# Starting one weight fewer before the wide products, and catching up inside them

## Chip, cores and metric

The kernel runs on one core of one Trainium2 chip. The metric is the device time of one execution in microseconds (us). Before the change it is 538.14 us, the median of three runs (537.76 to 539.08).

## What is computed

The reference is an attention with a decaying state, followed by two feed-forward layers on the 1536 tokens that it gives (B = 2, 768 positions, 8 heads of 64, so 512 features):

```python
for b in range(nb):                                  # blocks of 64 positions
    intra = einsum(einsum(qb, kb) * Dmask, vb)
    inter = einsum(qb * lam_pow, kv_state)
    out[:, :, sl] = intra + inter
    kv_state = lam_block * kv_state + einsum(kb_dec, vb)

rms = sqrt(mean(x * x) + 1e-06); xn = x / rms * rms_g     # layer 1: w_gate, w_val 512x1536, w_out 1536x512
x = (silu(xn @ w_gate) * (xn @ w_val)) @ w_out
h = maximum(maximum(x @ w1, x @ w2), x @ w3)              # layer 2: 512x768 each, w_out 768x512
return h @ w_out
```

## The kernel before

**Split weights.** Every large matrix product is made of three: an operand is cut into a high part (`wh`, `xh`) and what is left (`wl`, `xl`), and a product is high by high, high by low and low by high, each a TensorE (PE) matmul of 128x128 by 128x512. A weight is handled in pieces of 128 by 512, called units: `("g", f)` of w_gate, `("v", f)` of w_val, `("o", f)` of w_out; g0 below stands for `("g", 0)`. A unit comes as raw 32-bit words by DMA (`load_to`, L164 to L172: three DMAs for g and v, one for o) and is then made by four engines in turn:

- `begin_unit` (L231): two ScalarE (ACT) operations, `W<-wraw` (L252) and `wraw<-wraw` (L253);
- `words_of_unit` (L204), in three steps: three VectorE (DVE) operations `mid<-W` (L209), `mid<-mid` (L212), `W<-wraw,mid` (L216), and after the third an addition on GpSimd (POOL), `W<-W,wraw` (L219);
- `finish_unit` (L174): the cast `wh<-W` on ACT (L180) and the difference `wl<-W,wh` on POOL (L183). Only now can PE use the unit.

`third_of_unit` (L258) does this as a conveyor: one call in three begins a unit and does the first step of the one before it, the next finishes the one before that and does the second step, the third does the third step.

**Attention first, then mixed with the wide products.** Tokens come in 12 chunks of 128. The manual schedule at the end (L992 to L1018) runs seven turns, `s_` 0 to 6, of attention alone. In a turn the chunk `s_` is transposed (T: `pk`, `pq` on PE, then `kT`, `qT` on ACT), chunk `s_ - 1` gets its scores (C: `sc`, then `A` and the state `S` on DVE), chunk `s_ - 2` its output (M: `px` on PE, `sq` and `x` on ACT; U: `pm`) and chunk `s_ - 3` its scaling (N: `pb` on PE, `x` on DVE, `xh` on ACT; R: `xl` on POOL). The next chunk's `k`, `q`, `v` are loaded at T (`loads_at`, L104), and ahead of them the next unit's raw words (L995, L996). Units are begun at N of the late turns (L998 to L1000), and their steps are put behind b, U and V of the same turn.

After that `first_stage` (L656) begins the wide products of layer 1, for three blocks of 512 tokens: `hidden1` (L621) makes `pg` and `pv` of one f by `proj` (L492, 12 matmuls each), and after two f's `out_two` (L638) makes the four `acc`. The units are wanted in this order: g0, v0, g1, v1, g2, o0, o1, v2, g3, v3, o2, o3. What is left of the attention is spread between these matmuls: every third matmul calls `spread` (L467), directly or by `gap`. `spread` counts its calls in `pos["half"]`; it may call `third_of_unit` once, and then takes the next pieces of attention off their queue. Its first call also finishes the oldest unit and adds the last step of the one after it (L482 to L484). One `proj` has four such places, so g0 has places 1 to 4, v0 5 to 8, and o0 and o1 begin at place 21.

**Later stages.** When the attention is done (`lates`), `gap` (L453) runs the conveyor, and in `second_stage` (L895) products of sums of units (`Tg`, `Tv` and others) run in an order written out by hand.

**Order of waiting.** Each engine carries out its own instructions in the order in which the program emits them, so one that waits holds those behind it. PSUM tiles rotate through eight banks. SyncE (SP) issues all the DMAs of weights and chunks.

The lines touched are L469 in `spread`, and L995 and L998 in the schedule. The line that decides how often the conveyor moves during the first stage is

```python
if not lates and (pos["half"] - 1) % 5 % 3:
    third_of_unit()
```

which calls it at three places of five (the second, third and fifth).

Of the kernel before, what the change touches and what calls it, by code (L numbers as in the profile page):

```python
# [26 lines left out]
def tile_decay_attention_swiglu_maxout(  # L27
# [41 lines left out]
    lates = []  # L69
# [34 lines left out]
    def loads_at(c):  # L104
        if c <= CPNB:
            loads_to(c + 2)
        elif c == CPNB + 1:
            load(c + 1, 2)
        elif c + 1 < NCH:
            for n in range(3):  # L110
                load(c + 1, n)
# [50 lines left out]
    pos = {"load": 0, "made": 0, "raw": 0, "step": 0, "gap": 0, "half": 0, "quiet": False, "lag": 3, "narrow": True, "seam": False}  # L162
# [11 lines left out]
    def finish_unit(key, W, at):  # L174
        if key:
            if second_sum(key):
                W = sums_in.pop((key[0][1], key[1]))
            wh = wpools[at].tile([P, 512], F32R, tag="wh", name="wh")
            wl = wpools[at].tile([P, 512], F32R, tag="wl", name="wl")
            nc.scalar.copy(out=wh, in_=W.bitcast(F32))  # L180
            if second_sum(key):
                return lambda: lower_of_sum(key, W, wh, wl)
            nc.gpsimd.tensor_tensor(out=wl, in0=W.bitcast(F32), in1=wh.bitcast(F32), op=ALU.subtract)  # L183
            units[key] = (wh, wl)
# [73 lines left out]
    def third_of_unit():  # L258

        if not thirds:  # L260
            if pos["seam"] and stage1 and first_sum(stage1[0][0]):
                return
            done = stage2.pop(0) if stage2 else (None,) * 3
            unit = stage1.pop(0) if stage1 else (None,) * 5
            later = []
            thirds.extend([lambda: (begin_unit(), words_of_unit(0, *unit)),
                           lambda: (later.append(finish_unit(*done)), words_of_unit(1, *unit)),
                           lambda: (later[0] and later[0](), words_of_unit(2, *unit), stage2.append(unit[:3]))])
        thirds.pop(0)()
# [20 lines left out]
    def turn(c, scaled=True):  # L290
        kn, qn, vn = qkv[c][0], qkv[c][1], qkv[c][2]
        pk = bank("pk")
        pq = bank("pq")
        pkv = pk.rearrange("p (a t) -> p a t", t=P)
        pqv = pq.rearrange("p (a t) -> p a t", t=P)
        for a in range(NP):
            nc.tensor.transpose(pkv[:, a, :], kn[:, 2 * a:2 * a + 2, :].rearrange("p h d -> p (h d)"), ident)
        for a in range(NP):
            nc.tensor.transpose(pqv[:, a, :], qn[:, 2 * a:2 * a + 2, :].rearrange("p h d -> p (h d)"), ident)
        kT = att.tile([P, NP, P], F32, tag="kT", name="kT", bufs=1)  # L300
        nc.scalar.copy(out=kT, in_=pkv)
        qT = att.tile([P, NP, P], F32, tag="qT", name="qT", bufs=1)
        nc.scalar.copy(out=qT, in_=pqv)
        st[c] = dict(kT=kT, qT=qT, pq=pqv, vn=vn)
        if scaled:
            scaled_queries(c)
        if c == 0:
            decayed_keys(0)
# [26 lines left out]
    def masked(hf):  # L335
        def piece(c):
            d = st[c]
            if hf == 0:
                d["A"] = att.tile([P, H, C], F32, tag="A", name="A", bufs=1)
            nc.vector.tensor_tensor(  # L340
                out=d["A"].rearrange("p (a t) i -> p t a i", t=2)[:, hf],
                in0=d["sc"][hf][:, :HF].rearrange("p (a i) -> p a i", i=C),
                in1=Tm.rearrange("p (a t) i -> p t a i", t=2)[:, hf], op=ALU.mult)
            if hf == 0:
                d["S0"] = last_state[0]
                d["S1"] = next_state(c, 0, d["S0"])
        return piece
# [82 lines left out]
    def rest(c):  # L430
# [6 lines left out]
    named = dict(M=(2, mixed), N=(3, normed), C=(1, scores), a=(1, masked(0)), R=(3, rest),  # L437
                 b=(1, masked(1)), U=(2, summed), V=(1, advance), T=(0, lambda c: (loads_at(c), turn(c))),
                 t=(0, lambda c: (loads_at(c), turn(c, False))), Q=(1, scaled_queries),
                 K=(-1, decayed_keys), k=(0, decayed_keys),  # L440
                 w=(3, lambda c: None))
# [5 lines left out]
    def attn_step():  # L447
        _, fn, c = attn_q.pop(0)
        fn(c)
# [16 lines left out]

    def spread():  # L467
        pos["half"] += 1
        if not lates and (pos["half"] - 1) % 5 % 3:  # L469
            third_of_unit()  # L470
        if gaps[0]:
            left = sum(1 for p in attn_q if p[0] <= gaps[1])
            for _ in range(-(-left // gaps[0])):
                attn_step()
            gaps[0] -= 1
            if not attn_q and not lates:
                att_ctx.close()
                wpools.append(ctx.enter_context(tc.tile_pool(name="wp2", bufs=8)))
                lates.append(ctx.enter_context(tc.tile_pool(name="late", bufs=1)))
                pos["narrow"] = False  # L480
                x_sums()
        if pos["half"] == 1:  # L482
            finish_unit(*stage2.pop(0))
            words_of_unit(3, *split_unit[0])  # L484
# [479 lines left out]
    with tc.manual_schedule():  # L964
        nc.scalar.dma_start(out=lam8, in_=lam.rearrange("(o h) -> o h", o=1).to_broadcast([P, H]))
        loads_to(0)
        for to, src in crosswise(g_sb, rms_g.rearrange("(a p) -> p a", p=P)):
            nc.scalar.dma_start(out=to, in_=src)
        make_identity(nc, ident)
        nc.vector.memset(ones, 1.0)  # L970
        nc.vector.memset(zeros, 0.0)
        nc.scalar.activation(out=mhalf, in_=zeros[:, 0:1], func=AF.Silu)
        nc.vector.memset(mhalf, -0.5)
        warm = bank("warm")
        for i in range(9):
            nc.tensor.matmul(out=warm[:, 0:P], lhsT=zeros, rhs=zeros, start=True, stop=True)
        nc.vector.tensor_tensor(out=diag, in0=ident[:, :C], in1=ident[:, C:], op=ALU.add)
        for hf in range(2):
            nc.vector.tensor_copy(out=lamh[64 * hf:64 * hf + 64, :],
                                  in_=lam8.rearrange("p (a t) -> p t a", t=2)[64 * hf:64 * hf + 64, hf, :])  # L980
        for a in range(NP):
            nc.vector.tensor_tensor_scan(
                out=lami[:, a, :], data0=lamh[:, a:a + 1].to_broadcast([P, C]), data1=zeros[:, :C],
                initial=1.0, op0=ALU.mult, op1=ALU.add)
        for h in range(H):
            nc.vector.tensor_tensor_scan(
                out=Tm[:, h, :], data0=lam8[:, h:h + 1].to_broadcast([P, C]), data1=diag,
                initial=0.0, op0=ALU.mult, op1=ALU.add)
        loads_to(1)
        pos["narrow"] = False  # L990
        unit_ = None
        for s_ in range(CPNB + 3):  # L992
            while attn_q[0][0] == s_:
                fn = attn_q[0][1]
                if s_ and fn in (named["t"][1], named["T"][1]):  # L995
                    load_to(pos["load"] + 1)  # L996
                attn_step()
                if s_ > 2 and fn is named["N"][1]:  # L998
                    begin_unit()
                    unit_ = stage1.pop(0)  # L1000
                if unit_ and s_ == CPNB + 2:
                    if fn is named["U"][1]:
                        words_of_unit(3, *added_later)
                    elif fn is named["V"][1]:
                        for n in range(3):
                            words_of_unit(n, *unit_, split_add=True)
                        split_unit.append(unit_)
                        stage2.append(unit_[:3])
                elif unit_ and fn is named["b"][1]:
                    words_of_unit(0, *unit_)  # L1010
                elif unit_ and fn is named["U"][1]:
                    words_of_unit(1, *unit_)
                    if stage2:
                        finish_unit(*stage2.pop(0))
                elif unit_ and fn is named["V"][1]:
                    words_of_unit(2, *unit_, split_add=s_ == CPNB + 1)
                    added_later = unit_
                    stage2.append(unit_[:3])  # L1018
        begin_unit()
        finish = first_stage()  # L1020
        pos["step"] = len(steps)
        second_stage(finish)
# [31 lines left out]
```

## Time and profile before

| What | Value |
|---|---|
| median of 3 runs | 538.14 us (537.76 to 539.08) |
| profiled execution, its own time | 540.95 us |
| its span, first to last instruction | 539.2 us |
| mean granted TensorE clock | 0.994 of full |
| first wide matmul (`pg`) starts | 38.84 us |
| chain that ended last, share of PE | 84% |

The span is what the trace covers; the time of the same execution is 1.75 us longer. The views used below are the page's top, a table of stretches (busy time of each engine, granted clock as a share of full, DMA), the list of waits, and the instructions of one engine in order of time.

### The profile page before, as it was taken

To read this page: it belongs to the slowest core of one execution; us is meant where nothing else is said; L and a number is where in the kernel's file an instruction comes from. 1 tells how busy PE (TensorE), PEld (TensorE's weight loads), DVE (VectorE), ACT (ScalarE), POOL (GpSimd) and SP (SyncE) were. 2 spreads that over 40 slices of the span, in tenths; PEclk is the share of its full clock that TensorE was granted. 3 is DMA by queue.
4 is the path that set the end of the run, shared out by engine and by line. 5 is a ranking of instruction groups with operands and counts; after the bars stand their busy time and mean duration, and the time that the engine had idled before them with its cause. 6 is when DMAs were issued, how large, how long until landed. Compare 5 with 4: busy or idle time off the path is not lost.

```text
span 539.2 us, 9762 instructions
## 1 busy us (share of the span) xinstructions
PE 528.1 (98%) x3728; PEld 436.1 (81%) x3728; DVE 369.9 (69%) x680; ACT 278.2 (52%) x541; POOL 301.3 (56%) x247
## 2 busy tenths in 40 slices
PE   7989999999999999999999999999999999999997
PEld 6777777788888888888888888888888888888886
DVE  4795786538866677858667676878775587684354
ACT  3776684354463674364455446555466744641120
POOL 2485888334345667457365557985387543951060
PEclk9899999999999999999999999999999999999999
DMA  8989662001112213212131221211024321300014
GB/s 197 233 191 263 182 158 80 2 1 39 40 40 79 78 41 117 74 43 84 57 97 39 78 80 40 80 39 57 32 70 120 114 72 48 103 15 0 1 50 185
DMA packets 65598, 44.67 MB, mean 83 GB/s; under 512 B 40080, under 2 KB 61840, under 8 KB 65552
## 3 DMA queue, kind: packets, MB, share of 16 engines
q1 hardware_dynamic: 64848, 44.05, 28.4%
q8 instruction: 29, 0.48, 0.4%
q14 instruction: 17, 0.14, 0.1%
q10 hardware_dynamic: 704, 0.01, 0.1%
HBM read 40.90 MB, written 3.15 MB: 82 GB/s over the span
## 4 chain that ended last, share of the span: by engine, by line
PE 84%; DVE 1%; POOL 0%; issue 0%; ACT 0%; DVEq 0%
PE p L691 34%; PE acc L882 9%; PE r L691 9%; PE acc L488 6%; PE acc L490 6%; PE acc L489 6%; PE pv L498 5%; PE q L691 4%; PE pg L498 4%; PE px L384 1%; POOL wl L183 0%; PE sc L326 0%; PE sc L331 0%; PE pb L423 0%; DVE S L358 0%
## 5 line engine op out<-in xcount | busy, mean ns | idle before, releaser
L183 POOL TENSOR_TENSOR wl<-W,wh 128x512 fp32r<-128x512 f32 x77 | 102.1, 1326 | 53.1 <-ACT wh L180 53.0
L219 POOL TENSOR_TENSOR W<-W,wraw 128x512 int32<-128x512 int32 x60 | 79.1, 1318 | 75.9 <-DVE W L216 75.6
L180 ACT CAST wh<-W 128x512 fp32r<-128x512 f32 x77 | 47.9, 622 | 75.0 <-POOL W L219 73.7
L509 POOL TENSOR_TENSOR hl<-sg,hh 128x512 fp32r<-128x512 f32 x36 | 47.6, 1322 | 35.9 <-ACT hh L508 35.7
L691 PE MATMUL p<-xh,wh 128*128 128x512 f32 x148 | 57.6, 389 | 0.0
L691 PE MATMUL p<-xl,wh 128*128 128x512 f32 x148 | 57.6, 389 | 0.0
L691 PE MATMUL p<-xh,wl 128*128 128x512 f32 x148 | 57.6, 389 | 0.0
L490 PE MATMUL acc<-hh,wl 128*128 128x512 f32 x144 | 56.3, 391 | 0.5 <-POOL wl L183 0.5
L488 PE MATMUL acc<-hh,wh 128*128 128x512 f32 x144 | 56.7, 394 | 0.0
L489 PE MATMUL acc<-hl,wh 128*128 128x512 f32 x144 | 56.1, 389 | 0.0
L846 DVE TENSOR_TENSOR acc_sb<-acc,acc_sb 128x512 f32<-128x512 f32 x46 | 31.8, 690 | 17.4 <-PE acc L490 16.1
L252 ACT ACTIVATE W<-wraw 128x512 f32<-128x512 f32 x60 | 40.4, 673 | 3.9 <-DMA wraw<-in_moe_w_dram 3.9
L209 DVE TENSOR_SCALAR mid<-W 128x512 f32<-128x512 f32 x58 | 39.7, 684 | 3.3 <-ACT W L252 3.3
L212 DVE TENSOR_SCALAR mid<-mid 128x512 int32<-128x512 int32 x58 | 40.2, 693 | 0.8
L253 ACT ACTIVATE wraw<-wraw 128x512 int32<-128x512 uint32 x60 | 40.1, 669 | 0.0
L216 DVE SCALAR_TENSOR_TENSOR W<-wraw,mid 128x512 int32<-128x512 int32 x58 | 39.4, 679 | 0.9
L746 ACT COPY c<-p 128x512 f32<-128x512 f32 x34 | 19.9, 586 | 38.0 <-PE p L691 37.7
L509 POOL TENSOR_TENSOR hl<-m,hh 128x512 fp32r<-128x512 f32 x18 | 24.1, 1349 | 23.0 <-ACT hh L508 22.9
L691 PE MATMUL p<-yh,wh 128*128 128x512 f32 x90 | 35.0, 389 | 0.0
L691 PE MATMUL p<-yl,wh 128*128 128x512 f32 x90 | 35.0, 389 | 0.0
L691 PE MATMUL p<-yh,wl 128*128 128x512 f32 x90 | 35.0, 389 | 0.0
L508 ACT CAST hh<-sg 128x512 fp32r<-128x512 f32 x36 | 22.3, 620 | 24.0 <-DVE sg L632 16.4
(176 smaller groups left out, 1316.1 us busy)
## 6 DMA issues: line engine op xcount, KB each, us to landing
wraw<-in_moe_w_out_dram SPq DMA_DIRECT2D x18, 512.0 KB, 3.4
wraw<-in_moe_w_dram SPq DMA_DIRECT2D x18, 512.0 KB, 3.6
kn<-in_k_dram SPq DMA_DIRECT2D x12, 256.0 KB, 4.5
qn<-in_q_dram SPq DMA_DIRECT2D x12, 256.0 KB, 5.2
vn<-in_v_dram SPq DMA_DIRECT2D x12, 256.0 KB, 4.9
wraw<-in_moe_w_gate_dram SPq DMA_DIRECT2D x12, 256.0 KB, 3.4
wraw<-in_moe_w_gate_dram SPq DMA_DIRECT2D x24, 128.0 KB, 3.4
wraw<-in_moe_w_val_dram SPq DMA_DIRECT2D x12, 256.0 KB, 3.0
```

The source lines that it names most:

```text
L180: nc.scalar.copy(out=wh, in_=W.bitcast(F32))
L183: nc.gpsimd.tensor_tensor(out=wl, in0=W.bitcast(F32), in1=wh.bitcast(F32), op=ALU.subtract)
L212: nc.vector.tensor_scalar(out=mid[key], in0=mid[key], scalar1=0x07FFFFFF, scalar2=3, op0=ALU.bitwise_and, op1=ALU.logical_shift_left)
L219: nc.gpsimd.tensor_tensor(out=W, in0=W, in1=lo, op=ALU.add)
L252: nc.scalar.activation(out=W.bitcast(F32), in_=hi.bitcast(F32), func=AF.Abs)
L488: nc.tensor.matmul(out=out, lhsT=wh, rhs=xh_, start=first, stop=False)
L489: nc.tensor.matmul(out=out, lhsT=wh, rhs=xl_, start=False, stop=False)
L490: nc.tensor.matmul(out=out, lhsT=wl, rhs=xh_, start=False, stop=last)
L498: nc.tensor.matmul(out=ps, lhsT=w[:, kk * P:(kk + 1) * P], rhs=x[:, kk, :], start=n == 0, stop=n == len(todo) - 1)
L509: nc.gpsimd.tensor_tensor(out=dst_l, in0=src, in1=dst_h.bitcast(F32), op=ALU.subtract)
L691: nc.tensor.matmul(out=ps, lhsT=w[:, ks], rhs=r[:, o + k, :], start=first and k == 0 and n == 0, stop=k == 1 and n == 2, skip_group_check= ...
L882: nc.tensor.matmul(out=acc[:, cs], lhsT=x[:, ts], rhs=w[:, cs], start=n == 0, stop=n == len(todo) - 1)
```

## The change

Two places. In the attention turns the first raw unit is loaded from turn 2 on and not from turn 1 (L995), and units are begun at N of turns 4, 5, 6 and not of 3, 4, 5, 6 (L998); with the one begun behind the turns (L1019), four units are under way when the wide products begin, where there were five. In `spread`, up to the 24th place three of four places call the conveyor (the second, third and fourth); from the 25th on, three of five as before. Of the first 24 places that is 18 calls, where there were 14.

```diff
@@ spread
         pos["half"] += 1
-        if not lates and (pos["half"] - 1) % 5 % 3:
+        if not lates and ((pos["half"] - 1) % 4 if pos["half"] < 25 else (pos["half"] - 1) % 5 % 3):
             third_of_unit()
@@ the schedule
                 fn = attn_q[0][1]
-                if s_ and fn in (named["t"][1], named["T"][1]):
+                if s_ > 1 and fn in (named["t"][1], named["T"][1]):
                     load_to(pos["load"] + 1)
                 attn_step()
-                if s_ > 2 and fn is named["N"][1]:
+                if s_ > 3 and fn is named["N"][1]:
                     begin_unit()
                     unit_ = stage1.pop(0)
```

On PE no instruction moves. On the other engines the order changes from turn 1 on. First place: ACT behind the first two `proj`, before, from the cast of v1 on (`wh_1004<-W_809` is v1, `W_1065` is o1):

```order
L180 CAST wh_1004<-W_809 128x512
L629 ACTIVATE sg_1020<-pg_890 128x512
L301 COPY kT_1052<-pk_1042 128x512
L303 COPY qT_1054<-pq_1043 128x512
L252 ACTIVATE W_1065<-wraw_952 128x512
L253 ACTIVATE wraw_952<-wraw_952 128x512
L395 ACTIVATE sq_1097<-px0_1070 128x256
```

and now, from the cast of g1 on (`W_793` is g1, `W_873` is v1, `W_1024` is o0):

```order
L180 CAST wh_988<-W_793 128x512
L629 ACTIVATE sg_1006<-pg_876 128x512
L252 ACTIVATE W_1024<-wraw_938 128x512
L253 ACTIVATE wraw_938<-wraw_938 128x512
L301 COPY kT_1045<-pk_1035 128x512
L303 COPY qT_1047<-pq_1036 128x512
L180 CAST wh_1054<-W_873 128x512
L395 ACTIVATE sq_1086<-px0_1059 128x256
```

Each unit's cast stands one unit behind, and the cast of v1 now stands ahead of `sq`.

Second place: ACT one chunk later, before (`W_958` is o0) and now (`W_1199` is v2, `W_1024` is o0):

```order
L180 CAST wh_1199<-W_958 128x512
L629 ACTIVATE sg_1194<-pg_1123 128x512
L301 COPY kT_1239<-pk_1229 128x512
L303 COPY qT_1241<-pq_1230 128x512
L508 CAST hh_1246<-sg_1194 128x512
```

```order
L629 ACTIVATE sg_1185<-pg_1109 128x512
L252 ACTIVATE W_1199<-wraw_1020 128x512
L253 ACTIVATE wraw_1020<-wraw_1020 128x512
L180 CAST wh_1208<-W_1024 128x512
L301 COPY kT_1239<-pk_1229 128x512
L303 COPY qT_1241<-pq_1230 128x512
L508 CAST hh_1246<-sg_1185 128x512
```

The cast of o0 stood ahead of `kT` before too; now there is one more unit's begin in front of it.

Third place: POOL over the same chunk, before (`W_887` is g2, `W_958` o0, `W_1065` o1) and now (`W_873` is v1, `W_942` g2, `W_1024` o0, `W_1154` o1):

```order
L435 TENSOR_TENSOR xl_939<-x_798,xh_938 128x4x128
L219 TENSOR_TENSOR W_887<-W_887,wraw_741 128x512
L183 TENSOR_TENSOR wl_1110<-W_887,wh_1109 128x512
L509 TENSOR_TENSOR hl_1120<-sg_1020,hh_1119 128x512
L219 TENSOR_TENSOR W_958<-W_958,wraw_863 128x512
L414 TENSOR_TENSOR diag_82<-diag_82,mhalf_79 128x1
L287 TENSOR_TENSOR kd_1192<-kn_1036,Tm_80 128x512
L183 TENSOR_TENSOR wl_1200<-W_958,wh_1199 128x512
L435 TENSOR_TENSOR xl_939<-x_930,xh_938 128x4x128
L219 TENSOR_TENSOR W_1065<-W_1065,wraw_952 128x512
L509 TENSOR_TENSOR hl_1247<-sg_1194,hh_1246 128x512
L183 TENSOR_TENSOR wl_1309<-W_1065,wh_1308 128x512
```

```order
L219 TENSOR_TENSOR W_873<-W_873,wraw_725 128x512
L435 TENSOR_TENSOR xl_925<-x_782,xh_924 128x4x128
L183 TENSOR_TENSOR wl_1055<-W_873,wh_1054 128x512
L219 TENSOR_TENSOR W_942<-W_942,wraw_847 128x512
L509 TENSOR_TENSOR hl_1106<-sg_1006,hh_1105 128x512
L183 TENSOR_TENSOR wl_1170<-W_942,wh_1169 128x512
L414 TENSOR_TENSOR diag_82<-diag_82,mhalf_79 128x1
L219 TENSOR_TENSOR W_1024<-W_1024,wraw_938 128x512
L287 TENSOR_TENSOR kd_1183<-kn_1029,Tm_80 128x512
L435 TENSOR_TENSOR xl_925<-x_916,xh_924 128x4x128
L183 TENSOR_TENSOR wl_1209<-W_1024,wh_1208 128x512
L219 TENSOR_TENSOR W_1154<-W_1154,wraw_940 128x512
```

From the first `wl` of the wide stretch to that of o1 POOL has 17 operations before and 19 now: one addition and one difference more.

## Rows read from the trace of the kernel before

**Rows 1.** Top of the page: busy us of each engine, share, instructions.

```profile
PE 528.1 (98%) x3728; PEld 436.1 (81%) x3728; DVE 369.9 (69%) x680; ACT 278.2 (52%) x541; POOL 301.3 (56%) x247
```

**Rows 2.** Table of stretches: A:B us; busy (count) by engine; PEclk; DMA; GB/s.

```profile
17.40:18.50 1.10, 0.12 (x11) 0.04 (x4) 0.44 (x1) 1.10 (x4) 0.34 (x1) 1.00 0.80 239
21.00:24.50 3.50, 3.41 (x102) 2.89 (x95) 3.02 (x9) 2.08 (x8) 1.86 (x3) 0.51 0.81 212
24.50:33.00 8.50, 8.28 (x255) 7.36 (x248) 8.23 (x26) 7.70 (x19) 7.65 (x8) 1.00 0.79 185
34.00:38.10 4.10, 3.50 (x69) 2.90 (x69) 3.70 (x12) 3.61 (x10) 3.33 (x4) 1.00 0.75 182
38.10:41.60 3.50, 3.42 (x39) 2.49 (x39) 2.15 (x4) 2.09 (x4) 2.69 (x3) 0.51 0.97 251
46.10:68.00 21.90, 20.82 (x320) 16.30 (x318) 16.06 (x37) 15.19 (x35) 19.52 (x17) 1.00 0.81 223
92.00:539.00 447.00, 443.83 (x2130) 367.03 (x2128) 302.74 (x497) 217.09 (x401) 240.19 (x186) 1.00 0.19 61
```

**Rows 3.** List of PE's waits over the span: us in total, times, longest.

```profile
PE sc L331 <- issue: 1.0, 1, 1.0
PE px L384 <- issue: 0.8, 1, 0.8
PE pq L299 <- DMA qn<-in_q_dram: 0.6, 2, 0.4
PE acc L490 <- POOL wl L183: 0.5, 1, 0.5
PE px L384 <- ACT sg L629: 0.3, 1, 0.3
PE sc L331 <- DMA vn<-in_v_dram: 0.2, 1, 0.2
```

**Rows 4.** PE in order of time: start us, us, instruction, [idle before <- releaser].

```profile
46.65 0.39 PE L498 MATMUL pv<-xh,wl 128*128 128x512 f32 x1
...
49.89 0.28 PE L384 MATMUL px<-qs,S 64*64 64x64 f32 x3 [0.34 <-ACT sg L629]
...
67.99 0.50 PE L490 MATMUL acc<-hh,wl 128*128 128x512 f32 x1 [0.53 <-POOL wl L183]
...
199.00 0.39 PE L691 MATMUL r<-ah,wl 128*128 128x512 f32 x1
```

**Rows 5.** POOL in order of time: two of the differences wl, at 46 and 66 us.

```profile
46.13 1.30 POOL L183 TENSOR_TENSOR wl<-W,wh 128x512 fp32r<-128x512 f32 x1 [5.34 <-ACT wh L180]
...
66.65 1.29 POOL L183 TENSOR_TENSOR wl<-W,wh 128x512 fp32r<-128x512 f32 x1 [0.82 <-ACT wh L180]
```

**Rows 6.** POOL's groups, 46.1 to 67.97 us: count; busy us, mean ns; idle before.

```profile
L183 POOL TENSOR_TENSOR wl<-W,wh 128x512 fp32r<-128x512 f32 x5 | 6.4, 1289 | 7.6 <-ACT wh L180 7.6
L219 POOL TENSOR_TENSOR W<-W,wraw 128x512 int32<-128x512 int32 x4 | 5.2, 1309 | 0.0
L509 POOL TENSOR_TENSOR hl<-sg,hh 128x512 fp32r<-128x512 f32 x2 | 2.6, 1301 | 0.0
L435 POOL TENSOR_TENSOR xl<-x,xh 128x512 fp32r<-128x512 f32 x2 | 2.6, 1290 | 0.0
L287 POOL TENSOR_TENSOR kd<-kn,Tm 128x512 f32<-128x512 f32 x2 | 2.1, 1065 | 0.0
L414 POOL TENSOR_TENSOR diag<-diag,mhalf 128x1 f32<-128x1 f32 x2 | 1.1, 551 | 0.0
```

**Rows 7.** ACT and DVE in order of time, at sq, kT and the reduction.

```profile
51.81 0.68 ACT L395 ACTIVATE sq<-px 128x256 f32<-128x256 f32 x2
...
60.33 0.58 ACT L301 COPY kT<-pk 128x512 f32<-128x512 f32 x1
...
52.51 1.08 DVE L401 TENSOR_REDUCE zeros<-sq 128x128 f32<-128x512 f32 x1 [0.39 <-ACT sq L395]
```

**Rows 8.** POOL in order of time: the difference of unit Tg6, in the second stage.

```profile
193.61 1.30 POOL L183 TENSOR_TENSOR wl<-W,wh 128x512 fp32r<-128x512 f32 x1 [1.49 <-ACT wh L180]
```

## Prediction

> **What bounds the kernel now.** The top of the page comes first: PE is busy 528.1 us of 539.2 [rows 1]. So time can go only where PE stands still or where its clock is low, and the table of stretches says where. From 92 us to the end PE is busy 443.83 of 447.00 us at clock 1.00 [rows 2], with no wait long enough for the list. What can be won or lost lies in the first 92 us, where the change is. There the list of waits [rows 3] holds, beside those of the first 9 us, three kinds. Two stops are put down to "issue", 1.0 and 0.8 us: the engine waits for nothing that the profile shows. Two are for chunks that DMA brings late, 0.4 us for `qn` (the longer of its two) and 0.2 us for `vn`, both shortly ahead of 38.1 us. Two lie among the wide products: 0.34 us at 49.89 for the bank that the silu frees, and 0.53 us at 67.99, when the third matmul with o1 waits for its `wl` [rows 4]. PE is never held by the making of a weight before 38 us. Twice the granted clock is at half, the lower of its two levels (1.2 of 2.4 GHz): 3.5 us from 21.0 and 3.5 us from 38.1, each at 0.51, which costs 0.49 x 3.5 = 1.7 us of PE's work each time. The first follows a stretch with a stop (PE busy 0.12 of 1.10 us from 17.4). The second follows one with several (3.50 of 4.10 us from 34.0). No drop follows the stretch that is full, 24.5 to 33.0, with 8.28 of 8.50 [rows 2].
>
> What could become a bound is POOL: 19.52 of 21.90 us busy from 46.1 to 68.0 [rows 2]. The end of that stretch is just where PE waits for it.
>
> **The change, part by part.**
>
> *The weight that is no longer made in turn 3.* Its three ACT, three DVE and two POOL operations go from the attention turns. PE waits for none of them there [rows 3], so this alone gives 0. Its load of 512 KB goes as well: at 182 to 251 GB/s [rows 2] the chunks behind it in SP's queue come 2 to 3 us sooner, and the waits of 0.4 and 0.2 us ahead of 38.1 us go: **-0.6**. With them the stretch before 38.1 us becomes like the full one, and I take the half clock from 38.1 as gone: **-1.7**. The other end is 0, if other pauses lower it still.
>
> *The two "issue" stops.* They stand in the middle of runs of equal small matmuls, and PE's instructions keep their order, so I leave both, and the first drop of the clock: 0. The nearest rows bound it: nothing, or all of 1.0 + 0.8 + 1.7 = 3.5 us won, if lighter DMA traffic removes them. A loss from there is excluded, since the change takes DMA traffic out.
>
> *Start of the wide products.* The conveyor is one unit behind: the first place finishes v0, where it finished g1. Nothing in the order ahead of it moves, so v0's `wl` is made where g1's was, from 46.13 for 1.30 us, to 47.4 [rows 5]. PE wants it at 46.65 [rows 4]. That is a new wait of 0.8 us; the bank wait of 0.34 us behind it is then covered, so PE is 0.5 us late. Both are contained in the next step, which counts to one instant.
>
> *o1, wanted at the 22nd place.* The catch-up puts one more addition and one more difference ahead of o1's `wl` on POOL: 19 operations, not 17. **Lower end:** from 46.13 the 17 ended at 66.65 + 1.29 = 67.94, 21.81 us, of which 7.6 - 5.34 = 2.26 were waits for casts [rows 5, 6], so 19.55 of work. With 1.31 + 1.29 more it is 22.15. One wait for the cast of g1 stays as it was, half of what the row leaves beside its first and last, (2.26 - 0.82)/2 = 0.72. POOL cannot end before 46.13 + 22.87 = 69.0, 1.1 later than before.
>
> **Upper end:** the queues as they now stand. v1's addition is POOL's sixth operation, from 52.2 to 53.5 by the same rows, and ACT now holds v1's cast in front of `sq`, so `sq`, which began at 51.81 [rows 7], begins at 54.1. The reduction on DVE waits for it and starts 2.1 us later than 52.51, and behind it DVE has no gap. Next, o0's addition is POOL's thirteenth; with the steps above and a pause for the late `hh` it ends at 62.7. o0's cast waits for it in front of `kT`, which so begins at 63.4 and not at 60.33 [rows 7]. From there it is one chain across engines, each step at the 0.5 to 0.6 us from start to start that ACT's and DVE's operations have, 1.0 for the reduction: `qT` to 64.4, `qs` 65.1, `sg` 65.7, `hh` 66.3, `sq` 66.9, the reduction and two more DVE operations 69.1, `xh` 69.6, o1's cast 70.2, its `wl` 71.5. PE meets it with the matmul that ran at 67.99 [rows 4]: **+3.5**. `hl` on POOL, ready at 68.9, holds PE a little earlier in the same stop and adds nothing. I take the upper end. It walks the order as it stands, while the lower one lets no engine wait for another, against 7.6 us of such waits in POOL's largest group alone. Behind o1 the conveyor has caught up and stays a third ahead from place 25 on; o1 at 71.5 still leaves the later units several us: 0.
>
> At this stop the clock matters. A stop of 0.53 us in the same stretch left it at 1.00, and PE runs full-width matmuls on both sides [rows 2, 3]; the 0.8 us stop is followed by 4.1 us at 1.00. I take no drop. The Trainium skill, "TensorE: Matmul & The Clock Gate", Part 1, speaks against this: it says the clock is set to one of two levels by how busy the engine has lately been, and idle time lowers it. By that rule a stop of three us would be followed by half clock, and the sum below would be +2.9 and not +1.2. The trace agrees that stops come ahead of both drops, and shows no stop of this size amid wide products.
>
> *SP's queue.* A raw unit's DMAs now stand behind one more chunk's three. Units are still loaded a turn or more ahead of their begin: 0, and if one came late, its begin would hold ACT, which is part of the upper end.
>
> *Second stage.* The conveyor runs without units for a while, and starts again with another phase: the units of f = 4 to 7 come 12 wide matmuls later, those of f = 8 to 10 six earlier. The tightest is Tg6: its `wl` was there at 193.61 + 1.30 = 194.9 [rows 8] and was read at 199.00 [rows 4]. Twelve matmuls at 443.83 / 2130 = 0.21 us each [rows 2] are 2.5 us later, so it is ready at 197.4, still ahead: 0.
>
> **Sum:** -0.6 - 1.7 + 3.5 = **+1.2 us**. It is made on an execution whose own time is 540.95 (span 539.2), 2.8 above the median 538.14, as a profiled run is; the terms are differences, so they go on the median: **539.3**. That is 0.2%, within the 0.3% (1.6 us) that a measurement of this kernel can tell from no change.
>
> **The rivals.**
>
> *Slower: the clock falls at the o1 stop, or still falls at 38.1.* Either costs 1.7 us: 539.3 + 1.7 = **541.0**. For it: both drops came after stops far shorter than 3 us. Against: those stops lay among small matmuls. It decides when the stop at o1 passes from the 0.53 us that did no harm to about the 1.0 us that did [rows 2, 3].
>
> *Faster: the "issue" stops go with the load.* If they are late instructions behind busy DMA queues (DMA is 0.80 busy in the first stop [rows 2]), a lighter queue ends them: -3.5, **535.8**. Against: the load leaves the stream early, and other loads close up behind it.
>
> *POOL near its lower end.* +1.1 and not +3.5: **536.9**, on the line between no change and faster.
>
> **How the numbers follow.** Forecast 0.38; clock rival 0.34; issue rival 0.16; POOL at its lower end 0.12, half of it beyond the line. So faster 0.16 + 0.06 = 0.22, within 0.3% 0.38 + 0.06 = 0.44, slower 0.34. The range reaches from the issue rival, 535.6, to the clock rival, 541.2; left out are both drops together (542.7) and both gains together (533.4). The likeliest case alone spans 537.5 to 539.8.
>
> **What would show it.** Right: the `vn` and `qn` waits are gone from the list; the first wide matmul starts before 38.84; a new wait at v0 for POOL's `wl` of about 0.8 us; one at o1 of 2 to 3 us for `wl` or `hl`; POOL more than 90% busy between; clock 1.00 at the first `pg`; nothing new behind 92 us. Wrong: no new waits for `wl` among the wide products (then the change is a plain gain of 2 us or more), a low clock behind the o1 stop, or waits in the second stage.

## The result, and the profile after

The changed kernel takes 542.61 us, the median of six runs (541.42 to 543.50), where the kernel before takes 538.12 (six runs, 537.32 to 540.29): a ratio of 1.0066, 95% interval 1.0043 to 1.0089. The change is slower by 0.4 to 0.9%. Forecast were 539.3 us and "no change"; the range ended at 541.2. Medians and ratios in this document are of fast runs; the one slow run is of e8_early, at 1063.65 us.

The profiled execution takes 542.72 us, close to its median. Its list of TensorE's (PE's) waits answers to [rows 3]:

```profile
PE acc L488 <- ACT wh L180: 1.9, 1, 1.9
PE pv L498 <- POOL wl L183: 0.6, 1, 0.6
PE acc L490 <- POOL wl L183: 0.6, 1, 0.6
PE pv L498 <- ACT wh L180: 0.6, 1, 0.6
PE pq L299 <- DMA qn<-in_q_dram: 0.5, 2, 0.3
PE sc L331 <- issue: 0.4, 1, 0.4
```

Of the two "issue" stops of 1.0 and 0.8 us one of 0.4 is left, and the wait for `vn` is gone. New are three waits for weights: two at v0 (`pv`) and the one of 1.9 us at o1 (`acc`, for the cast `wh`); the one for o1's `wl` was in [rows 3] with 0.5 us. In PE's rows in order of time, the first wide matmul, v0, o0's first matmul, and o1:

```profile
35.48 0.47 PE L498 MATMUL pg<-xh,wh 128*128 128x512 f32 x1
...
42.69 0.50 PE L498 MATMUL pv<-xh,wh 128*128 128x512 f32 x1 [0.56 <-ACT wh L180]
...
44.06 0.50 PE L498 MATMUL pv<-xh,wl 128*128 128x512 f32 x1 [0.64 <-POOL wl L183]
...
63.93 0.39 PE L488 MATMUL acc<-hh,wh 128*128 128x512 f32 x1
...
67.32 0.51 PE L488 MATMUL acc<-hh,wh 128*128 128x512 f32 x1 [1.91 <-ACT wh L180]
...
68.69 0.58 PE L490 MATMUL acc<-hh,wl 128*128 128x512 f32 x1 [0.63 <-POOL wl L183]
```

The first wide matmul starts at 35.48 us, where the profile of before has 38.84. At o1 PE stands still for 1.91 us, waiting for the cast `wh`, and for 0.63 us, waiting for `wl`. POOL's rows of the differences of v0 and o1:

```profile
42.72 1.29 POOL L183 TENSOR_TENSOR wl<-W,wh 128x512 fp32r<-128x512 f32 x1 [4.22 <-ACT wh L180]
...
67.35 1.29 POOL L183 TENSOR_TENSOR wl<-W,wh 128x512 fp32r<-128x512 f32 x1 [1.70 <-ACT wh L180]
```

The table of stretches, with the columns of [rows 2]:

```profile
21.00:24.50 3.50, 3.50 (x111) 3.24 (x112) 2.32 (x8) 2.73 (x9) 1.79 (x2) 1.00 0.77 202
38.10:41.60 3.50, 3.49 (x76) 2.51 (x75) 1.85 (x3) 2.73 (x9) 0.39 (x1) 1.00 0.84 194
46.10:68.00 21.90, 19.23 (x304) 14.09 (x302) 15.54 (x33) 15.98 (x36) 18.81 (x17) 1.00 0.78 204
68.90:72.40 3.50, 3.50 (x9) 2.72 (x9) 3.37 (x9) 1.74 (x4) 3.50 (x4) 0.51 0.35 101
92.00:534.00 442.00, 441.78 (x2175) 365.51 (x2175) 302.83 (x496) 219.19 (x403) 240.59 (x187) 1.00 0.19 60
```

Both stretches at half clock of before are at 1.00 now; a new one, at 0.51 (1.2 of 2.4 GHz), follows the stop at o1. From 92 us on PE is busy 441.78 of 442.00: nothing is lost in the second stage.

PE's order is the same in both kernels, so single matmuls can be compared. The first wide one is 3.4 us earlier than in the profile of before, the first with o2 (92.12 us before, 94.05 now) is 1.9 us later, and the times of the two executions differ by 1.8. The medians differ by 4.5. What the profiled execution of before had that its median run has not is the first question.

### The profile page after: what moved, and what is told of

The parts are those of the page before. It is cut to its first block, busy times and chain, and to the rows that moved or that the text cites. A ratio compares the mean times of both kernels' runs of the same rounds, so it can differ in the third digit from the quotient of the medians.

```text
span 540.9 us, 9746 instructions
## 1 busy us (share of the span) xinstructions
PE 528.0 (98%) x3728; PEld 434.9 (80%) x3728; DVE 371.2 (69%) x680; ACT 279.7 (52%) x541; POOL 300.9 (56%) x247
## 4 chain that ended last, share of the span: by engine, by line
PE 90%; POOL 3%; DMA 3%; issue 2%; DVE 1%; SPq 0%; ACT 0%; POOLq 0%; DVEq 0%
PE p L691 34%; PE acc L882 9%; PE r L691 9%; PE acc L488 6%; PE acc L490 6%; PE acc L489 6%; PE pv L498 5%; PE pg L498 5%; PE q L691 4%; PE px L384 2%; POOL W L219 1%; DMA wraw<-in_moe_w_out_dram 1%; DMA qn<-in_q_dram 1%; POOL kd L287 1%; PE sc L331 1%
## 5 line engine op out<-in xcount | busy, mean ns | idle before, releaser
L183 POOL TENSOR_TENSOR wl<-W,wh 128x512 fp32r<-128x512 f32 x77 | 100.7, 1309 | 59.5 <-ACT wh L180 59.5
L219 POOL TENSOR_TENSOR W<-W,wraw 128x512 int32<-128x512 int32 x60 | 80.6, 1343 | 72.2 <-DVE W L216 68.0
L488 PE MATMUL acc<-hh,wh 128*128 128x512 f32 x144 | 57.5, 399 | 1.9 <-ACT wh L180 1.9
L509 POOL TENSOR_TENSOR hl<-m,hh 128x512 fp32r<-128x512 f32 x18 | 24.1, 1342 | 23.0 <-ACT hh L508 22.9
L488 PEld LDWEIGHTS acc<-hh,wh 128*128 128x128 f32 x144 | 27.3, 190 | 7.6 <-ACT wh L180 2.0
```

The lines of the kernel that those rows point to most:

```text
L219: nc.gpsimd.tensor_tensor(out=W, in0=W, in1=lo, op=ALU.add)
L488: nc.tensor.matmul(out=out, lhsT=wh, rhs=xh_, start=first, stop=False)
L509: nc.gpsimd.tensor_tensor(out=dst_l, in0=src, in1=dst_h.bitcast(F32), op=ALU.subtract)
```

## The experiments

One table for all; each ratio is against the kernel before, run beside it on the same chip. "Start" is the first wide matmul in the run's profile, "stretch" the time from there to the first matmul with o2.

| Run | Under way, edit | Median us | Ratio (95%) | Start us | Stretch us |
|---|---|---|---|---|---|
| (profile before) | five | 538.12 | | 38.84 | 53.3 |
| e1_before | five, none | 538.76 | 0.998 (0.9953 to 1.0007) | 36.16 | 53.1 |
| e2_load | five, later load | 540.09 | 1.0014 (0.999 to 1.0038) | 36.83 | 54.4 |
| e4_catch | five, catch-up | 542.78 | 1.0056 (1.0029 to 1.0083) | 37.21 | 57.5 |
| (profile after) | four, catch-up | 542.61 | 1.0066 (1.0043 to 1.0089) | 35.48 | 58.6 |
| e12_after | four, catch-up | 543.03 | 1.0088 (1.0059 to 1.0117) | 36.87 | 56.3 |
| e6_order | four, thirds last | 544.25 | 1.0081 (1.0053 to 1.0109) | 36.62 | 59.8 |
| e5_wl_dve | four, two `wl` on VectorE | 544.99 | 1.0119 (1.0088 to 1.0151) | 34.87 | 61.4 |
| e7_late | four, catch-up late | 547.60 | 1.0152 (1.0124 to 1.018) | 35.01 | 59.6 |
| e8_early | four, catch-up early | 544.25 | 1.0096 (1.007 to 1.0121) | 34.88 | 61.6 |
| e10_fill | four, stop filled | 543.79 | 1.0089 (1.0066 to 1.0112) | 38.31 | 56.4 |
| e14_cast | four, o1's cast earlier | 540.70 | 1.0027 (1.0009 to 1.0044) | 35.11 | 56.3 |
| e9_silu | five, silu first | 537.85 | 0.9988 (0.9968 to 1.0008) | 36.43 | 52.2 |
| e11_silu_first | five, silu ahead of cast | 537.89 | 0.9981 (0.9961 to 1.0000) | 39.90 | 51.0 |
| e13_silu_again | the same again | 536.60 | 0.9965 (0.9942 to 0.9988) | 36.37 | 51.4 |

A stretch at half clock inside it lengthens the time: in the profile before 2.7 us of the one from 38.1 us lie there, which cost 1.3 us, and in the profile after all 3.5 us of the one from 68.9 us, which cost 1.7 (both at 0.51; estimates).

### The kernel before, again

No edit.

> The kernel before, unchanged, with the granted clock of every run. Theory A (the clock's drops explain why the medians moved by 4.5 us where the two profiled executions moved by 1.8): runs of before fall on steps of 1.0 to 1.7 us by how many drops to half clock they hold; the median, near 538, has one drop or none (mean clock 0.997 or more), and runs near 540 to 541 two (0.994). Rival B (a profiled execution is about 2.8 us longer than an unprofiled one of the same kernel, whatever the clock): runs near 538 show two drops (0.994) as the profile did. Ratio to before 1.000 either way.

A second profile of the same kernel. Its list of waits, PE's first wide matmul, and the one stretch at half clock:

```profile
PE px L384 <- ACT sg L629: 1.1, 1, 1.1
PE warm L976 <- DVE zeros L971: 1.1, 1, 1.1
PE sc L331 <- POOL kd L287: 1.1, 1, 1.1
PE sc L326 <- ACT qT L303: 0.7, 1, 0.7
PE acc L490 <- POOL wl L183: 0.6, 1, 0.6
```

```profile
36.16 0.48 PE L498 MATMUL pg<-xh,wh 128*128 128x512 f32 x1
```

```profile
8.90:12.40 3.50, 3.50 (x64) 3.05 (x64) 1.85 (x7) 1.07 (x2) 1.93 (x2) 0.51 1.10 283
```

No "issue" stop is listed, no wait for `vn` or `qn`, and the only half clock lies at 9 us. The change moves only the first load there (issued at 8.69 us), and with it moved e12_after, below, has the same half clock. This execution takes 538.10 us, less than the median of its own kernel's runs, so a profiled execution is not longer as such: rival B falls. Theory A holds for the medians, while single runs scatter (541.64 us at 0.997). Over the 96 runs of before that stand beside the experiments, 28 have a mean granted clock of 0.999 or more (median 538.2 us), 50 of 0.996 to 0.998 (539.1), 18 of 0.994 or less (540.9). The profile on which the prediction was made, at 0.994, is of the last kind. A mean doesn't tell where a drop lies, but the traces do: of the seven with five units under way only that one has half clock from 38.1 us. What the change would take away there is absent from the others.

### One part alone

The later load alone: L995 changed, L998 and L469 as before.

> The load shift alone: the first raw unit is loaded from turn 2 on; five units are still begun ahead of the wide products, and the conveyor is as before. Theory A (the traffic of that load is what holds the instructions of TensorE and the late chunks): the first wide matmul starts 2 to 4 us earlier in the profile than 38.84, the two stops put down to issue shrink from 1.8 to under 0.6 us in sum, no half clock ahead of 42 us; time 536 to 537.5 where before is 538.1. Rival B (the earlier start comes from the unit that is no longer made in turn 3): first wide matmul within 1 us of 38.84, time 537.8 to 538.6.

No difference that can be measured. The profile has an "issue" stop of 1.1 us and half clock from 20.9 us, and the first wide matmul at 36.83: these stops come without that load's traffic too. Theory A falls.

The catch-up alone: L469 changed, five units under way.

> The catch-up alone: three places of four to the 24th call the conveyor, with five units under way as before. Theory A (the stops among the wide products come from four units only, the conveyor being one unit behind): v0 and o1 are made earlier than wanted, no wait for a weight over 0.6 us, time 537.5 to 538.5. Rival B (the denser conveyor itself holds ScalarE's and VectorE's queues, so that the attention's steps between the wide products come late): waits of 1 us or more among the wide products for sg, kT, zeros or hh, time 539.5 to 541.

The catch-up costs as much alone as the whole change does, so the start with one unit fewer gives nothing back that the ratios can tell. No wait for a unit exceeds 0.7 us; there are many small ones for the attention, of which PE's rows in order of time show three:

```profile
62.52 0.46 PE L423 MATMUL pb<-ident,diag 128*128 128x128 f32 x2 [0.54 <-ACT kT L301]
...
72.37 0.50 PE L488 MATMUL acc<-hh,wh 128*128 128x512 f32 x1 [0.68 <-DVE W L216]
74.15 0.40 PE L384 MATMUL px<-qs,S 64*64 64x64 f32 x11 [0.56 <-DVE S L358]
```

Half clock follows from 75.0 to 78.4 us. Theory B holds in kind: with denser thirds in the queues of ScalarE (ACT) and VectorE (DVE) the attention comes late. Of its single waits of 1 us or more there is only one, 1.1 us for `sg`, which e1_before has as well. (Four units under way without a catch-up is no kernel: o1 would be finished by the conveyor's 14th call, at place 23, and is read from place 21 on.)

### The change again, and its stop filled

> The change, unchanged, with the granted clock of every run, beside the two runs below. Theory A (the drop behind the stop at o1 belongs to most executions of the change, and the waits alone cost the rest): median 0.5 to 0.9% over before; runs at clock 1.000 stand 2.5 to 3.5 us over runs of before at 1.000, the others 1 to 2 us higher. Rival B (nearly all of the loss is the clock): runs of both at 1.000 within 1 us of each other.

```profile
36.87 0.48 PE L498 MATMUL pg<-xh,wh 128*128 128x512 f32 x1
...
67.75 0.50 PE L488 MATMUL acc<-hh,wh 128*128 128x512 f32 x1 [1.91 <-ACT wh L180]
```

```profile
68.90:72.40 3.50, 3.28 (x15) 2.66 (x16) 3.38 (x10) 2.55 (x5) 3.50 (x5) 1.00 0.23 63
```

The same 1.91 us at o1, and this time no half clock behind it; the one that this execution has lies at 9 us, as in e1_before. So the waits alone lengthen the stretch from 53.12 to 56.25 us, by 3.1. The drop at o1 is a matter of the single execution. Of the change's twelve runs (in both groups) one has a clock of 0.999 or more, five 0.996 to 0.998, six 0.994 or less; their medians, 541.4, 542.5 and 543.3 us, are 3.2, 3.4 and 2.4 over those of before at the same clock. So most of the loss is there at equal clock: rival B falls. The second half of theory A holds. The first half, that the drop behind o1 belongs to most executions, isn't shown: a mean clock doesn't tell where the drop lies, and of the five profiles with a stop of 1.8 us or more at o1 three have it (the profile after, and e6_order and e5_wl_dve, both from 68.6 to 75.4 us) and two don't (e12_after and e7_late).

The stop filled:

```diff
@@ out_two
                 wh, wl = units["o", f]
+                if j == 0 and f == 1 and m == 0:
+                    for _ in range(9):
+                        nc.tensor.matmul(out=ps, lhsT=nought.to_broadcast([P, P]), rhs=two[0][1], start=False, stop=False)
```

> The change, with nine matmuls of a zero weight by hh, adding nothing, put ahead of the first matmul with o1: they take the 1.9 us in which TensorE stood still there. Theory A (standing still lowers the clock): the wait for o1's cast falls to under 0.4 us, o1's matmul starts when it did, and no half clock follows; 1 to 1.7 us less than the change in most runs. Rival B (the clock falls there for another reason, such as the work around the stop): half clock as before behind it, same time as the change or up to 0.5 us more.

The matmuls fill the stop, o1 is as late as before, and no half clock follows in the profile; but in e12_after none did either. Its stretch is as long as there, 56.4 and 56.3 us. Its six runs have clocks of 0.994 to 0.997. The edit also adds a copy that makes the zero weight, and the start of this profile differs (the wait for `kd` 2.1 us, half clock from 9.2 to 16.0 us), so the time tells nothing. Inconclusive.

### Why o1 is late

The thirds behind the attention's pieces:

```diff
@@ spread
-        if not lates and ((pos["half"] - 1) % 4 if pos["half"] < 25 else (pos["half"] - 1) % 5 % 3):
-            third_of_unit()
+        turn_ = not lates and ((pos["half"] - 1) % 4 if pos["half"] < 25 else (pos["half"] - 1) % 5 % 3)
...
+        if turn_:
+            third_of_unit()
         if pos["half"] == 1:
```

> The change, but at each place the conveyor's third comes behind the pieces of attention and not ahead of them, so that a cast of a unit stands behind kT and qT on ScalarE. Theory A (o1 is late by a chain over ScalarE and VectorE, in which o0's cast holds kT, qT, hh, sq and so o1's own cast; POOL stood idle 1.7 us ahead of o1's difference): the stop at o1 falls from 2.5 us to 1.5 us or less, and with it in most runs the half clock behind it; time 538.5 to 541. Rival B (POOL's work is the bound): o1's difference ends no earlier, stop 2.2 to 3 us, time 542 to 543.5.

The stop stays (2.4 us for the cast), and the time rises. The edit missed its aim: its profile still has a cast that waits 2.28 us for POOL ahead of `kT` (at 60.14 and 60.67 us). It doesn't tell the two theories apart.

Two differences on VectorE:

```diff
@@ finish_unit
+            eng = nc.vector if key in (("g", 2), ("o", 0)) else nc.gpsimd
-            nc.gpsimd.tensor_tensor(out=wl, in0=W.bitcast(F32), in1=wh.bitcast(F32), op=ALU.subtract)
+            eng.tensor_tensor(out=wl, in0=W.bitcast(F32), in1=wh.bitcast(F32), op=ALU.subtract)
```

> The change, with the differences wl of g2 and o0 made on VectorE and not on POOL, which takes 2.6 us off POOL between v0's and o1's wl and adds 1.2 to 1.4 us to VectorE. Theory A (POOL's work is the bound of that stretch): o1's wl ends 2 to 2.6 us earlier against the first wide matmul, the stop at o1 falls from 2.5 us to under 0.8, time about 539.5 to 540.5 on a chip where before is 538 to 540. Rival B (the chain over ScalarE and VectorE and the order in their queues): VectorE's extra work gives back what POOL saves, stop at o1 still 1.5 us or more, time within 0.3% of the change.

POOL's row of o1's difference (its line is 184 here):

```profile
68.74 1.29 POOL L184 TENSOR_TENSOR wl<-W,wh 128x512 fp32r<-128x512 f32 x1 [2.74 <-ACT wh L180]
```

POOL, 2.6 us of work lighter, only waits longer for the cast, 2.74 us where it was 1.70; the stop at o1 is 1.9 us again, and VectorE's extra work adds a wait of 1.3 us. POOL's work is not the bound: rival B, and slower than it expected.

The catch-up elsewhere, all places from 16 to 20, and all places from 1 to 8, in place of three in four:

```diff
-((pos["half"] - 1) % 4 if pos["half"] < 25 else (pos["half"] - 1) % 5 % 3)
+(15 < pos["half"] < 21 or (pos["half"] - 1) % 5 % 3)
```

```diff
-((pos["half"] - 1) % 4 if pos["half"] < 25 else (pos["half"] - 1) % 5 % 3)
+(pos["half"] < 9 or (pos["half"] - 1) % 5 % 3)
```

> Four units under way, but the catch-up is packed late: three places of five as before, and only places 16 to 20 all call the conveyor, so 14 calls by the 20th place. Theory A (what costs is that one and a third units more are made between 42 and 68 us, wherever): as slow as the change, 0.5 to 0.8% over before, with a stop at o1 of 2 us or more. Rival B (the density of three in four over the whole stretch costs, by holding the attention's steps at each place): waits ahead of o1 go, and the whole costs 0.2 to 0.4%.

> Four units under way, and the catch-up packed early: all of the first eight places call the conveyor, then three of five. Theory A (the work is what costs): as slow as the change, 0.5 to 0.8% over before. Rival B (it matters where the work stands): POOL and VectorE, idle 4.2 and 3.7 us at the first places, take it in; o1 is made by its time, no stop over 0.8 us there, 0.0 to 0.3% over before; the price would be raw words that come late at the start (waits of ScalarE for wraw of 1 us or more).

Packed late is slower still than the change; packed early isn't told from it (1.0096 against 1.0066 and 1.0088). Packed late, PE waits for units all along: 0.65 us at v0, 1.21 at g2, 2.4 at o1, and 2.6 at one of the later `pv`. Packed early, all is lost at once and nothing after:

```profile
43.84 0.35 PE L410 MATMUL pm<-ones,zeros 128*128 128x1 f32 x2 [3.48 <-DVE zeros L401]
...
46.09 0.79 PE L498 MATMUL pv<-xh,wh 128*128 128x512 f32 x1 [1.10 <-ACT wh L180]
...
49.52 0.80 PE L498 MATMUL pv<-xh,wl 128*128 128x512 f32 x1 [2.21 <-POOL wl L183]
```

The attention's reduction comes 3.5 us late and v0's parts 3.3, with half clock from 44.9 to 55.1 us; o1 is then in time. The work is nearly the same in both (14 and 15 calls by the 20th place); where it stands sets how much of it PE sees. Packed late, both theories fail by the size (0.5 to 0.8 and 0.2 to 0.4% expected, 1.2 to 1.8 measured), though theory A's stop of 2 us or more at o1 is there. Packed early, rival B is right that o1 comes in time and wrong on the cost (0.0 to 0.3% expected, 0.7 to 1.2 measured), which the end of theory A's range still meets.

One cast. In every run above with four units under way and o1 late, o1's cast stands on ACT behind another unit's begin and `xh`; in e8_early, where o1 is in time, it stands ahead of `xh`. In ACT's rows of the changed kernel, in order of time, from o0's cast to o1's:

```profile
59.67 0.62 ACT L180 CAST wh<-W 128x512 fp32r<-128x512 f32 x1 [1.54 <-POOL W L219]
60.20 0.58 ACT L301 COPY kT<-pk 128x512 f32<-128x512 f32 x1
...
62.62 0.62 ACT L508 CAST hh<-sg 128x512 fp32r<-128x512 f32 x1 [1.36 <-DVE sg L632]
63.14 0.65 ACT L395 ACTIVATE sq<-px 128x256 f32<-128x256 f32 x2
63.68 1.14 ACT L397 ACTIVATE x<-px,g_sb 128x128 f32<-128x128 f32 x4
64.68 0.71 ACT L252 ACTIVATE W<-wraw 128x512 f32<-128x512 f32 x1
65.24 0.71 ACT L253 ACTIVATE wraw<-wraw 128x512 int32<-128x512 uint32 x1
66.13 0.62 ACT L427 CAST xh<-x 128x512 fp32r<-128x512 f32 x1 [0.19 <-DVE x L425]
66.66 0.61 ACT L180 CAST wh<-W 128x512 fp32r<-128x512 f32 x1
```

and POOL's row of o1's words in the same profile:

```profile
63.07 1.33 POOL L219 TENSOR_TENSOR W<-W,wraw 128x512 int32<-128x512 int32 x1
```

The words are there at 63.07 + 1.33 = 64.40; the cast starts at 66.66, behind the begin of another unit and `xh`. So the last experiment on this moves that one cast:

```diff
@@ spread
-        pos["half"] += 1
+        pos["half"] += 1; pos["half"] == 18 and finish_unit(*stage2.pop(0))
```

> The change, with o1's cast moved three instructions forward on ScalarE, ahead of a unit's two begin operations and of xh; nothing moves on any other engine. Theory A (the place of the cast in ScalarE's queue is the stop): the cast runs 1.9 us sooner against the first wide matmul, o1's difference on POOL then stands behind hl alone and ends 1.7 us sooner, the stop at o1 falls from 2.5 us to 0.8 or less; time 541 to 541.8 where before is 538.1 to 539, ratio 1.0045 to 1.0060. Rival B (PE waits for a chain in which the cast is only one of several late ones): the stop moves to xh, hl or xl and the time stays at 542.5 to 543.

```profile
64.50 0.65 ACT L180 CAST wh<-W 128x512 fp32r<-128x512 f32 x1
65.00 0.71 ACT L252 ACTIVATE W<-wraw 128x512 f32<-128x512 f32 x1
65.58 0.70 ACT L253 ACTIVATE wraw<-wraw 128x512 int32<-128x512 uint32 x1
66.13 0.64 ACT L427 CAST xh<-x 128x512 fp32r<-128x512 f32 x1
```

```profile
66.75 0.50 PE L490 MATMUL acc<-hh,wl 128*128 128x512 f32 x1 [0.74 <-POOL wl L183]
...
72.37 0.40 PE L384 MATMUL px<-qs,S 64*64 64x64 f32 x11 [0.54 <-DVE S L358]
```

The cast runs 2.0 us sooner against o0's first matmul (0.76 us behind it, 2.73 in e12_after), the stop is 0.74 us where it was 2.54, and one wait of 0.54 us comes back behind it. The ratio falls to 1.0027, below what theory A expected. Theory A is shown for most of the stop: it is that cast's place in the queue. The stretch is no shorter than in e12_after, 56.3 us, since PE reaches v0 later in this profile, 7.4 us behind the first wide matmul and not 6.2. Nine of the twelve runs have a clock of 1.000, where the change has one of twelve. That fits "TensorE: Matmul & The Clock Gate", Part 1, of the Trainium skill, which says that idle time of the engine lowers the clock. It isn't shown that the stop alone sets it: of the 16 runs of before beside them, a kernel whose two profiles wait 0.5 and 0.6 us at o1, only seven have 0.999 or more. At that clock the nine runs are 2.0 us over these seven (540.4 and 538.5), where the change was 3.2 over.

### A version that beats both

In e1_before PE waits 1.1 us for the bank that the silu frees, and the silu stands behind v1's cast, which waits for POOL:

```profile
45.72 0.62 ACT L180 CAST wh<-W 128x512 fp32r<-128x512 f32 x1 [1.51 <-POOL W L219]
46.25 0.59 ACT L629 ACTIVATE sg<-pg 128x512 f32<-128x512 f32 x1
```

First try: the silu ahead of the third at the same place.

```diff
@@ proj
-                spread()
                 if n == 2 and then:
                     then()
+                spread()
```

> The kernel before, with the silu of a pg put ahead of the conveyor's third at the same place, so that on ScalarE it doesn't stand behind a cast that waits for POOL. Theory A: the wait for sg in g0's successor (0.3 to 1.1 us at 47 to 50 us) goes, and nothing takes its place: 0.1 to 0.2% faster than before. Rival B: the cast and the difference behind the silu come 0.5 us later, v1 or o1 is late by as much: no difference, ratio 0.999 to 1.001.

The wait is still there (0.8 us): v1's cast is emitted at place 3, the silu at place 5, so the two kept their order. Ratio 0.9988, not told from no change. Second try: the same, and the call of place 3 left out and one put in at place 6. The second call, which finishes v1, so moves from place 3 to place 5, and the third from 5 to 6.

```diff
@@ spread, with the edit above
-        if not lates and (pos["half"] - 1) % 5 % 3:
+        if not lates and (pos["half"] - 1) % 5 % 3 and pos["half"] != 3 or pos["half"] == 6:
```

> The kernel before, with the silu put ahead of the conveyor's third as in the run with the silu first, and the second call moved from place 3 to place 5, the third to place 6: so the silu of the first pg does stand ahead of v1's cast, which waits 1.5 us for POOL. Theory A: the wait for sg at 46 to 50 us (0.3 to 1.1 us) goes and v1 is still in time; 0.1 to 0.3% faster than before. Rival B: kT and qT, and so the next product of scores, still stand behind the cast, and PE waits there for the same time a little later: ratio 0.999 to 1.001.

> The kernel before with the silu ahead of v1's cast, a second time, since the first ratio (0.9981, 0.9961 to 1.0000) leaves it open by a hair. Theory A (the waits for sg and for o1's wl, 1.1 and 0.6 us in the kernel before, are gone for good): ratio 0.997 to 0.9985 again, and from the first wide matmul to 92 us no wait of TensorE over 0.3 us. Rival B (chance of the runs): ratio 0.999 to 1.001.

```profile
43.97 0.57 ACT L629 ACTIVATE sg<-pg 128x512 f32<-128x512 f32 x1
45.60 0.62 ACT L180 CAST wh<-W 128x512 fp32r<-128x512 f32 x1 [1.06 <-POOL W L219]
46.12 0.58 ACT L301 COPY kT<-pk 128x512 f32<-128x512 f32 x1
```

These rows of e13_silu_again have the silu ahead of the cast, and PE's wait for `sg` is gone; the longest wait left behind the first wide matmul is 0.4 us, for o1's `wl`. The stretch is 51.0 and 51.4 us in the two profiles, 2.1 and 1.7 less than in e1_before. The two ratios are 0.9981 (0.9961 to 1.0000) and 0.9965 (0.9942 to 0.9988): faster than before by 0.1 to 0.6% in the second group of runs, and so faster than both kernels. At a clock of 0.999 or more they take 537.2 and 536.4 us, and before takes 538.1 and 538.0 beside them, so the gain isn't the clock's alone.

## Why the prediction was wrong

**-0.6 and -1.7 ahead of 38.1 us: wrong.** The failing step is "the terms are differences, so they go on the median". The waits for `vn` and `qn` and the half clock from 38.1 us belonged to that one execution, 2.8 us over its median, a gap that was put down to "as a profiled run is"; e1_before has neither and takes 538.10 us, and the changed kernel still waits 0.2 us for `qn` at 35.1 us. How much of a gain there is ahead of the wide products isn't settled. The first wide matmul starts at 36.16 to 39.90 us in the seven profiles with five units under way and at 34.87 to 36.87 in the seven with four (e10_fill left out). At v0's first matmul, where PE waits for v0, little of it is left: 42.69 and 43.11 us in the two profiles of the change, 42.39 in e1_before (42.4 to 46.2 in the seven with five).

**The "issue" stops, left at 0: half right.** They are neither fixed nor caused by the load: 1.0 and 0.8 us in one profile of before, none in the other, 0.4 and 1.0 in sum in two of the change, 1.1 with the load alone. The rival that priced their end at -3.5 us falls.

**v0, a new wait of 0.8 us: right.** 1.2 us in the first profile of the change, 0.64 in the second.

**o1, +3.5 us: right in size.** The chain was walked from v0's difference at 46.13 us to the end of o1's at 71.5, 25.4 us; measured are 42.72 to 67.35 + 1.29 = 68.64, 25.9 us. Its steps hold too: `kT` begins 17.5 us behind v0's difference where 17.3 was said, o1's difference 24.6 (24.1). Counted from the first wide matmul, the third matmul with o1 comes at 33.2 and 32.3 us in the two profiles of the change, at 29.2 and 29.0 in those of before: 3.1 to 4.2 us later. What the chain didn't show is which of its steps can be moved: o1's words wait 2.3 us for their cast, and the last run on the stop takes 1.8 of its 2.5 us away by moving that one cast. The rival of POOL's lower end falls with the run on VectorE.

**The clock behind it, no drop: wrong in part.** This was the rival with a chance of 0.34. Half clock follows the stop at o1 in one of the two profiles of the change. Over its twelve runs the mean clock is 0.9946, over before's 96 it is 0.9968; 0.0022 of 540 us is 1.2 us (an estimate), and how much of that lies behind o1 stays open. At equal clock the change is 2.4 to 3.4 us slower; with 1.2 that is 3.6 to 4.6, where the medians moved by 4.5 and, in e12_after, by 4.0 (543.03 against 539.06).

**SP's queue and the second stage, 0: right.** PE is busy 441.78 of 442.00 us from 92 us on.

So the forecast missed by a credit of 2.3 us, which e1_before, an execution near the median, had nowhere to give, and in part by the clock; what was to be +1.2 us is 2.4 to 3.4 at equal clock. The slower rival named the right mechanism but was stacked on the same credit, and ended at 541.0. The case of both drops together, 542.7, which the range left out, comes close to the 542.61 measured; that is partly luck, since the drop at 38.1 us that it keeps is in no profile of the change.

## What to carry to other kernels

Before a stop or a stretch at half clock is counted as something to win, look whether the profiled execution is the median one: where its own time lies over the median by as much as the gain sought, the gain may be that execution's luck. In this kernel, work moved out of a stretch with slack into one where every engine's queue feeds the next costs by its place in the queues, not by its busy time: five placements of the same work, against one start, cost between 0.3 and 1.5%. When a weight comes late, look for the instructions that stand ahead of its cast although its operands have long been there; moving one instruction gave time back here, and taking 2.6 us of work off POOL, at VectorE's expense, gave none.

## What the runs showed of the hardware

One kernel's executions differ ahead of 42 us by where PE stops for nothing that the profile shows (none in e1_before, 1.8 us in sum in the profile before; up to 2.4 us, in e11_silu_first) and by whether its clock falls to half there (from 8.9 us in e1_before, from 21.0 and 38.1 in the profile before, not at all in e9_silu). The half clock lasted 3.4 us in e4_catch, 6.8 in e5_wl_dve and e6_order and 10.2 in e8_early. The same stop of 1.91 us was followed by it in one profile of the change and not in the other.

The "issue" stops are not spread at random. In the 15 profiles they stand at five places of PE's order only, behind some 706, 961, 1218, 1473 and 1730 of its instructions (matmuls and weight loads), 255 to 257 apart. All 22 of them (0.2 to 1.3 us long) end 1.3 to 1.6 us after a 16 KB packet of the instruction queue q8 has ended. Which of the five places costs something, and how much, differs from execution to execution. That PE waits there for its next instructions is likely by this, but no run tests it.
